# Dummy products in fp32, a re-ordered attention start and re-ordered loads in a fused attention and gated feed-forward kernel

## The chip, the cores and the metric

One core of a Trainium2 chip. The metric is the device time of one execution in microseconds (us). A profile is one execution; its span is 1.7 to 1.8 us shorter than the time that is measured for the same execution.

Names used here: PE is TensorE (matrix products), PEld its weight loads, DVE VectorE, ACT ScalarE, POOL GpSimd. POOL also issues the loads that convert fp32 in memory to bf16 on chip.

## The reference, cut to what matters

```python
# q, k, v: (8 batches, 8 heads, 1024, 64); E, F: (64, 1024)
k_proj = einsum('ks,bhsd->bhkd', E, k)
v_proj = einsum('ks,bhsd->bhkd', F, v)
scores = q @ k_proj^T / 8
attn   = exp(scores - max) / sum          # the kernel leaves the max out
x      = (attn @ v_proj) as (8192, 512)
g      = x @ w_gate                       # 512 x 1536
out    = (g * sigmoid(g)) * (x @ w_val) @ w_out
```

## The kernel before

The rows are cut into 16 chunks of 512. Each chunk goes through 12 steps f of the gate and val products (g and v, 128 columns of the weights each, 512 rows) and through the y products with `w_out`. The attention of later chunks is spread between these products. Only the start differs: nothing can be multiplied with the weights until the first chunk's attention is done, and that is a chain of small steps on four engines. It begins with turning E (to turn is to transpose, on PE) and projecting K, and the chunk is taken in two halves of 256 rows to start sooner.

The names in the code and in the profiles: the chunk's attention is cut into four parts, u = 0 to 3 (two groups of four heads, each for two halves of the rows). Each part has its scores, their exponentials ee, and AA, which is ee divided by its row sums (one multiplication with the reciprocals rr). AT is AA turned; BD and BDV hold the projections of K and V; P V is the product of BDV and AT; its turned result xT is the input of the gate and val products.

```python
ps_g, ps_v: 2 PSUM banks each;  ps_y: 1 bank;  ps_a: 3 banks      # banks "g", "v", "y", "a"

def load_w_gv(c0, c1, which=(0, 1)):      # one load of gate, one of val, issued by POOL
    ...
def u_V0(p0, p1, at):                     # V's projection for head pairs p0..p1 of batch 0
    t = bank(at, [P, p1 - p0, P], FP32, "kvp")
    matmul(out=t, lhsT=zeros[:, 0:P], rhs=zeros[...], start=True, stop=False)   # zero product
    for j in range(NJ):
        for c in range(2):                # two column halves of the array
            matmul(out=t[64*c:64*c+64, :, 64*c:64*c+64], lhsT=FT[:, j, :], rhs=..., start=False, ...)
    nc.scalar.copy(out=BDV[0][:, p0:p1, :], in_=t[:])

def warm(n):                              # n dummy products, to release the clock
    ps = bank("v", [P, CW], FP32, "warm")
    for _ in range(n):
        matmul(out=ps[:], lhsT=zeros[:, 0:P], rhs=zeros[:], start=True, stop=True)   # bf16, 512 columns

# the start, in program order (loads on POOL, everything else as named)
load_q(0, 0, (2, 4)); load F; load_v(0, (0, 4, 6, 8)); load_w_gv(0, 1); load_w_gv(1, 2, (0,))
warm(11); turn(0, "v"); warm(4)           # turn(0): E, turn(1): F
... K's first four heads: casts, u_KV, u_T, u_KT0, warm(1)
u_S(0, 0); u_R(0, 0); u_N(0, 0)           # scores+exp (PE, ACT), sum (DVE), scale = AA (POOL)
load_w_gv(1, 2, (1,)); load_w_gv(2, 4, (0,))
u_T(0, 2); warm(2); K's other heads; warm(1); u_KT0((2, 4)); u_T(0, 1); u_T(0, 3)
u_S(0, 2); u_R(0, 2); u_N(0, 2); turn(1, "a", (0,))
u_S(0, 1); u_R(0, 1); u_N(0, 1); turn(1, "a", (1,))
u_S(0, 3, "v"); u_R(0, 3)
u_A(0, 0, act); u_N(0, 3, dve)            # u_A: turn AA, copy by the named engine
u_V0(0, 2, "y"); u_PV2(0, 0, 0, 0, act); u_V0(2, 3, "y"); u_A(0, 2, act); u_V0(3, 4, "v")
u_PV1(...pair 2); u_A(0, 1, dve); u_PV1(...pair 3); u_A(0, 3, act)
load_w_gv(2, 4, (1,))
f_mm(0, 0, 0, 0); u_PV2(...); f_mm(0, 0, 1, 0); f_mm(0, 1, 0, 0); u_PV2(...); f_mm(0, 1, 1, 0)
load_w_gv(4, 6); load_q(0, 1, hs=(0, 4)); load_w_gv(6, 8); load_q(0, 1, hs=(4, 8)); load_w_gv(8, 10) ...
```

The softmax here doesn't subtract the row's maximum and nothing guards it: scores larger than these inputs give would overflow.

## Time and profile before

| | before |
|---|---|
| median of the first runs (568.65 to 569.04) | 568.66 us |
| span of the profile | 566.9 us |
| PE busy | 560.2 us, 99% |
| start of the third val product (T) | 25.93 us |
| start of the val product of f=6 | 33.29 us |
| DMA rate 22 to 30 us | 196 to 197 GB/s |

In a timeline line the first number is the start in us, the second the stretch in us; then come engine, line, operation, output and inputs, and how many instructions were merged. A bracket tells how long the engine was idle before and what ended it. In the view by stretches, a row has the stretch, its length and the busy time of PE, PEld, DVE, ACT and POOL with the number of instructions, then the granted clock, the DMA share and the DMA rate in GB/s. These are rows of before, first K's first projection, the first gate product and the third val product (T) from the timeline, then three stretches:

```profile
8.16 1.06 PE L150 MATMUL kvp<-kb,ET 128*64 128x256 bf16 x8
...
20.70 0.60 PE L377 MATMUL gps<-xT,wg 128*128 128x256 bf16 x4
...
25.93 1.03 PE L377 MATMUL vps<-xT,wv 128*128 128x512 bf16 x4
```

```profile
20.00:22.00 2.00, 1.82 (x21) 1.52 (x19) 1.19 (x3) 0.96 (x2) 2.00 (x4) 1.00 1.58 191
22.00:24.00 2.00, 1.98 (x19) 1.62 (x18) 1.28 (x4) 0.88 (x2) 2.00 (x4) 1.00 1.45 197
24.00:26.00 2.00, 1.90 (x14) 1.17 (x13) 1.56 (x3) 0.90 (x2) 1.37 (x2) 1.00 1.45 196
```

Before, the DMA rate stays at 191 GB/s or more from 20 to 30 us.

### The profile page before, as it was taken

To read this page: it belongs to the slowest core of one execution; us is meant where nothing else is said; L and a number is where in the kernel's file an instruction comes from. 1 tells how busy PE (TensorE), PEld (TensorE's weight loads), DVE (VectorE), ACT (ScalarE), POOL (GpSimd) and SP (SyncE) were. 2 spreads that over 40 slices of the span, in tenths; PEclk is the share of its full clock that TensorE was granted. 3 is DMA by queue.
4 is the path that set the end of the run, shared out by engine and by line. 5 is a ranking of instruction groups with operands and counts; after the bars stand their busy time and mean duration, and the time that the engine had idled before them with its cause. 6 is when DMAs were issued, how large, how long until landed. Compare 5 with 4: busy or idle time off the path is not lost.

```text
span 566.9 us, 7938 instructions
## 1 busy us (share of the span) xinstructions
PE 560.2 (99%) x2970; PEld 266.3 (47%) x2970; DVE 339.2 (60%) x576; ACT 236.0 (42%) x417; POOL 110.4 (19%) x124
## 2 busy tenths in 40 slices
PE   8999999999999999999999999999999999999997
PEld 4654444444444444444444444444444444444444
DVE  3786664766476645766466655666547665545550
ACT  3664352444435433443434434354343543443222
POOL 6851250124012400124002230023100220000000
PEclk9999999999999999999999999999999999999999
DMA  9999989729913795029940499105990214100012
GB/s 201 194 200 188 175 126 199 141 57 187 192 50 74 113 196 119 38 57 163 183 83 37 76 185 204 38 19 101 200 183 20 57 38 75 38 37 32 25 38 93
DMA packets 111159, 62.78 MB, mean 111 GB/s; under 512 B 64272, under 2 KB 102416, under 8 KB 111120
## 3 DMA queue, kind: packets, MB, share of 16 engines
q0 software_dynamic: 42896, 29.49, 36.1%
q1 hardware_dynamic: 67392, 31.46, 26.2%
q10 hardware_dynamic: 832, 1.31, 0.8%
q8 instruction: 23, 0.38, 0.3%
q14 instruction: 16, 0.13, 0.1%
HBM read 60.29 MB, written 16.78 MB: 136 GB/s over the span
## 4 chain that ended last, share of the span: by engine, by line
PE 97%; ACT 1%; DVE 1%; issue 0%
PE gps L377 29%; PE yps L415 29%; PE vps L377 29%; PE kvp L150 3%; PE sc L271 2%; PE pv L328 2%; PE warm L513 1%; ACT ee L275 0%; ACT AT L138 0%; DVE BD L138 0%; ACT th L389 0%; PE qTp L237 0%; PE efp L501 0%; PE aTp L317 0%; PE pv L343 0%
## 5 line engine op out<-in xcount | busy, mean ns | idle before, releaser
L396 DVE SCALAR_TENSOR_TENSOR s<-th,gps 128x512 f32<-128x512 f32 x192 | 130.3, 679 | 134.4 <-ACT th L389 134.0
L377 PE MATMUL gps<-xT,wg 128*128 128x512 bf16 (+1 forms) x776 | 197.6, 377 | 0.1
L377 PE MATMUL vps<-xT,wv 128*128 128x512 bf16 (+1 forms) x776 | 197.5, 377 | 0.0
L415 PE MATMUL yps<-wo,hT 128*128 128x512 bf16 (+1 forms) x780 | 194.5, 376 | 0.0
L389 ACT ACTIVATE th<-gps 128x512 f32<-128x512 f32 x192 | 114.6, 597 | 159.0 <-PE gps L377 153.9
L401 DVE TENSOR_TENSOR hT<-s,vps 128x512 bf16<-128x512 f32 x192 | 131.9, 687 | 20.4 <-DVE s L396 0.5
L301 POOL TENSOR_TENSOR AAd<-ee,rr 128x512 bf16<-128x512 f32 x56 | 58.2, 1041 | 342.5 <-issue 180.6
L415 PEld LDWEIGHTS <-hT 128*128 128x128 bf16 x780 | 76.2, 98 | 89.9
L377 PEld LDWEIGHTS <-wv 128*128 128x128 bf16 x776 | 74.0, 98 | 83.3 <-issue 2.9
L377 PEld LDWEIGHTS <-wg 128*128 128x128 bf16 x776 | 74.0, 98 | 81.3 <-issue 1.2
L425 ACT ACTIVATE ysb<-yps 128x512 f32<-128x512 f32 (+1 forms) x65 | 38.4, 590 | 77.7 <-PE yps L415 77.7
L138 ACT CAST xT<-pv 128x512 bf16<-128x512 f32 (+1 forms) x62 | 35.9, 581 | 52.5 <-PE pv L328 50.3
L286 DVE TENSOR_REDUCE zz<-ee 128x8 f32<-128x512 f32 x64 | 43.4, 679 | 22.1 <-ACT ee L275 22.1
L275 ACT ACTIVATE ee<-sc 128x512 f32<-128x512 f32 x64 | 38.2, 597 | 19.8 <-PE sc L271 18.7
L271 PEld LDWEIGHTS <-qTd 128*128 128x128 bf16 x224 | 17.2, 98 | 13.2 <-DMA qTd<-qb 0.2
L328 PE MATMUL pv<-AT,BDV 128*128 128x512 bf16 x60 | 22.4, 379 | 0.1
L271 PE MATMUL sc<-BD,qTd 128*128 128x128 bf16 x224 | 21.6, 219 | 0.0
L288 DVE RECIPROCAL rr<-zz 128x8 f32<-128x8 f32 x64 | 13.0, 203 | 6.6 <-DVE zz L286 0.5
L108 POOL DMA_DIRECT2D qb<-in_q_dram x18 | 16.3, 907 | 1.4 <-POOLq L651 0.8
L150 PE MATMUL kvp<-kb,ET 128*64 128x512 bf16 (+1 forms) x72 | 15.5, 358 | 0.0
L162 DVE CAST BDV<-kvp 64x256 bf16<-64x256 f32 x7 | 3.0, 426 | 20.0 <-ACT ks L158 17.8
L150 PE MATMUL kvp<-vb,FT 128*64 128x512 bf16 x56 | 13.4, 382 | 0.0
(66 smaller groups left out, 137.6 us busy)
## 6 DMA issues: line engine op xcount, KB each, us to landing
out_dram<-ysb SPq DMA_DIRECT2D x63, 256.0 KB, 2.3
qb<-in_q_dram POOLq DMA_DIRECT2D x14, 512.0 KB, 18.1
kb<-in_k_dram POOLq DMA_DIRECT2D x7, 1024.0 KB, 11.0
vb<-in_v_dram POOLq DMA_DIRECT2D x7, 1024.0 KB, 14.5
wo<-in_moe_w_out_dram POOLq DMA_DIRECT2D x2, 768.0 KB, 21.9
wg<-in_moe_w_gate_dram POOLq DMA_DIRECT2D x5, 256.0 KB, 8.4
wv<-in_moe_w_val_dram POOLq DMA_DIRECT2D x5, 256.0 KB, 9.0
kraw<-in_k_dram ACTq DMA_DIRECT2D x2, 512.0 KB, 4.9
```

The source lines that it names most:

```text
L138: (nc.scalar.copy if eng is nc.scalar else eng.tensor_copy)(out=out, in_=in_)
L150: nc.tensor.matmul(out=t[lo : lo + 64, h0:h1].rearrange("p h d -> p (h d)"), lhsT=w[:, j, :], rhs=src[b][:, h0:h1, j, :], start=(j == 0), ...
L271: nc.tensor.matmul(out=ps[:, n, :], lhsT=t[:, n, :], rhs=BD[b % 2][:, 4 * g + n, :], start=True, stop=True)
L275: nc.scalar.activation(out=e[:].rearrange("p h j k -> p (h j k)"), in_=ps[:].rearrange("p a k -> p (a k)"), func=AF.Exp, scale=scale,)
L286: nc.vector.reduce_sum(out=z[:], in_=e[:], axis=AX.X)
L301: eng.tensor_tensor(out=a.rearrange("p j h k -> p h j k"), in0=ee.pop((b, u))[:], in1=rr.pop((b, u))[:].unsqueeze(3).to_broadcast([P, 4, 2 ...
L377: nc.tensor.matmul(out=ps[:, ts], lhsT=(wg, wv)[w][:, kt, f * P : (f + 1) * P], rhs=x[:, kt, ts], start=(kt == 0), stop=(kt == NKT - 1),)
L389: nc.scalar.activation(out=th[:], in_=ps[:], func=AF.Tanh, scale=0.5)
L396: nc.vector.scalar_tensor_tensor(out=s1[:], in0=th[:], scalar=1.0, in1=g[:], op0=ALU.add, op1=ALU.mult)
L401: nc.vector.tensor_tensor(out=hT[c][:, f, :], in0=s1[:], in1=ps[:], op=ALU.mult)
L415: nc.tensor.matmul(out=yy[c][:, cs], lhsT=hT[c][:, f, i * P : (i + 1) * P], rhs=wo[:, f, cs], start=(f == 0), stop=(f == NFT - 1),)
L425: nc.scalar.activation(out=ysb[:, cs], in_=yy[c][:, cs], func=AF.Copy, scale=0.5)
```

## The change

Its intent is to shorten the start. The dummy products become a few long fp32 ones, presumably to have fewer instructions. Half of F's turn moves ahead into a dummy's place, with its copy on DVE. V's projection for the first two pairs becomes a wide form without the zero product (a memset on DVE in the first microseconds clears the target instead) and stands ahead of P V. The fourth AA moves from DVE to POOL and one copy from ACT to DVE. The third g is put in y's idle bank. The weights of f=2 and f=3 are loaded apart, those of f=3 behind the fourth AA on POOL, and the second half of the second chunk's q goes ahead of the weights of f=6 and 7.

```diff
+    def u_V0w(p0, p1, at):
+        t = bank(at, [P, p1 - p0, 2, D], FP32, "kvp")
+        for j in range(NJ):
+            nc.tensor.matmul(out=t[64:P]..., lhsT=FT[:, j, :], rhs=vb[0][:, 2 * p0 : 2 * p1, j, :], ...)
+        for c in range(2):
+            nc.scalar.copy(out=BDV[0][rows, p0:p1, rows], in_=t[64:P, :, c, :])
 ...
-            half[c, f, w] = bank("gv"[w], [P, CW], FP32, "gv"[w] + "ps")
+            where = "y" if (c, f, w) == (0, 2, 0) else "gv"[w]
+            half[c, f, w] = bank(where, [P, CW], FP32, where + "ps")
 ...  (warm(n): one fp32 product of min(64 n, 512) columns where n >= 4; its zeros come
      from a new fp32 memset; later warm(1) and warm(2) become warm(4) and warm(4))
-        warm(11)
+        for n in (8, 8, 4):
+            warm(n)
         turn(0, "v")
-        warm(4)
+        warm(8)
 ...
-        load_w_gv(2, 4, (0,))
+        load_w_gv(2, 3)
 ...
-        warm(1)                          # after K's other heads
+        turn(1, "a", (0,), dve)
 ...
+        turn(1, "a", (1,))               # ahead of the scores of u=2
-        turn(1, "a", (0,))               # and both turns of F out of their old places
-        turn(1, "a", (1,))
         u_S(0, 3, "v")
         u_R(0, 3)
+        u_N(0, 3)
+        load_w_gv(3, 4)
         u_A(0, 0, act)
-        u_N(0, 3, dve)
-        u_V0(0, 2, "y")
+        u_V0w(0, 2, "y")
+        u_V0(2, 3, "v")
         u_PV2(0, 0, 0, 0, act)
-        u_V0(2, 3, "y")
-        u_A(0, 2, act)
-        u_V0(3, 4, "v")
+        u_A(0, 2, dve)
+        u_V0(3, 4, "y")
 ...
+        f_mm(0, 0, 0, 0)                 # ahead of u_A(0, 3)
         u_A(0, 3, act)
-        load_w_gv(2, 4, (1,))
-        f_mm(0, 0, 0, 0)
 ...
         load_q(0, 1, hs=(0, 4))
+        load_q(0, 1, hs=(4, 8))
         load_w_gv(6, 8)
-        load_q(0, 1, hs=(4, 8))
```

More of the change, by code (lines that the diff above doesn't have):

```diff
@@ L185, in u_V0 @@
         nc.scalar.copy(out=BDV[0][:, p0:p1, :], in_=t[:])
+    def u_V0w(p0, p1, at):
+        t = bank(at, [P, p1 - p0, 2, D], FP32, "kvp")
+        for j in range(NJ):
+            nc.tensor.matmul(
+                out=t[64:P].rearrange("p a c d -> p (a c) d"),
+                lhsT=FT[:, j, :],
+                rhs=vb[0][:, 2 * p0 : 2 * p1, j, :],
+                start=(j == 0),
+                stop=(j == NJ - 1),
+            )
+        for c in range(2):
+            rows = slice(64 * c, 64 * c + 64)
+            nc.scalar.copy(out=BDV[0][rows, p0:p1, rows], in_=t[64:P, :, c, :])
     def u_KT(b, at="a", prs=(0, NPAIR)):
@@ L490 @@
         load_k(0, 4, 8)
-        zeros = const.tile([P, CW], BF16, name="zeros")
+        zero32 = const.tile([P, CW], FP32, name="zero32")
+        nc.vector.memset(zero32[:], 0.0)
+        zeros = const.tile([P, 2 * P], BF16, name="zeros")
         nc.vector.memset(zeros[:], 0.0)
@@ L495, with turn @@
         nc.vector.memset(ks[0][64:P], 0.0)
-        def turn(which, at, halves=(0, 1)):
+        nc.vector.memset(BDV[0][:, 0:2], 0.0)
+        def turn(which, at, halves=(0, 1), eng=nc.scalar):
             for half in halves:
@@ L506, in turn @@
                 js = slice(4 * half, 4 * half + 4)
-                copy(nc.scalar, (ET, FT)[which][:, js, :], ps[:])
+                copy(eng, (ET, FT)[which][:, js, :], ps[:])
         def warm(n):
             ps = bank("v", [P, CW], FP32, "warm")
-            for _ in range(n):
+            z = zeros if n < 4 else zero32
+            for _ in range(n if n < 4 else 1):
                 nc.tensor.matmul(
-                    out=ps[:], lhsT=zeros[:, 0:P], rhs=zeros[:],
+                    out=ps[:, 0 : min(64 * n, CW) if n >= 4 else 2 * P],
+                    lhsT=z[:, 0:P],
+                    rhs=z[:, 0 : min(64 * n, CW) if n >= 4 else 2 * P],
                     start=True, stop=True,
@@ L537 @@
         u_KT0((0, 2), "vg", (dve, dve, dve, act))
-        warm(1)
+        warm(4)
         u_S(0, 0, "g")
@@ L542 @@
         load_w_gv(1, 2, (1,))
-        load_w_gv(2, 4, (0,))
+        load_w_gv(2, 3)
         u_T(0, 2, "a", act)
-        warm(2)
+        warm(4)
         u_KV(0, "k", (4, 8), at="y")
-        warm(1)
+        turn(1, "a", (0,), dve)
         u_KT0((2, 4), "vg", (dve, dve, act, act))
```

## The prediction

> **What bounds the kernel now.** I read the page first: its busy line, its slices and the chain that ended last.
>
> ```profile
> PE 560.2 (99%) x2970; PEld 266.3 (47%) x2970; DVE 339.2 (60%) x576; ACT 236.0 (42%) x417; POOL 110.4 (19%) x124
> PE   8999999999999999999999999999999999999997
> PE 97%; ACT 1%; DVE 1%; issue 0%
> ```
>
> TensorE is the bound: 97% of the chain is its own work, and only the first slice (14.2 us) has an 8. The waits by window say the same: from 25 us on, TensorE has no wait on another engine, and the stretches 60 to 530 us are 100% busy. The change touches no product after the start, so it can move the time only through the moment at which the dense stream begins. I call that moment **T**: the start of the third val product (f=2, 512 columns), 25.93 us now. From there each f costs 1.73 us (25.07 to 26.80) without a gap. T earlier by x makes the kernel faster by x, unless a transfer stops the stream later.
>
> Next I read the timeline from 0 to 35 us, then the waits of TensorE there. Whatever precedes T is a chain of short steps over four engines:
>
> ```profile
> 1.20 4.88 PE L513 MATMUL warm<-zeros 128*128 128x512 bf16 x11 [1.20 <-DVE zeros L492]
> 6.12 1.07 PE L501 MATMUL efp<-ident_fp,Eraw 64*128 64x64 f32 x8
> ...
> 15.43 0.37 ACT L138 COPY FT<-efp 128x256 bf16<-128x256 bf16 x1
> ...
> 16.17 0.39 ACT L138 COPY FT<-efp 128x256 bf16<-128x256 bf16 x1
> ...
> 16.56 0.64 PE L178 MATMUL kvp<-vb,FT 128*64 128x128 bf16 x16
> ...
> 17.38 0.45 ACT L185 CAST BDV<-kvp 128x256 bf16<-128x256 f32 x1
> ...
> 17.88 0.39 PE L343 MATMUL pv<-AT,BDV 128*128 128x256 bf16 x2 [0.68 <-ACT BDV L185]
> ```
>
> The reader is to see two copies of F's turn on ACT among the exponentials, and P V waiting 0.68 us for the V projection's copy on the same engine. ACT runs without pause from 14.94 to 17.83 us in the chain.
>
> The third view is the issue list, taken around single issues, beside the timeline's issue times. It gives landings: issue plus time to landing.
>
> ```profile
> wv<-in_moe_w_val_dram POOLq DMA_DIRECT2D x1, 128.0 KB, 12.5
> ```
>
> ```profile
> 8.65 0.75 POOL L118 DMA_DIRECT2D wv<-in_moe_w_val_dram  x1
> 21.36 0.60 PE L377 MATMUL vps<-xT,wv 128*128 128x256 bf16 x4
> ...
> 22.34 0.42 PEld L377 LDWEIGHTS <-wv 128*128 128x128 bf16 x4
> ...
> 33.29 1.03 PE L377 MATMUL vps<-xT,wv 128*128 128x512 bf16 x4
> ```
>
> So the first val weights land at 8.65 + 12.5 = 21.15 us and are used from 21.25 us: **no slack**. Likewise gate f=1 lands at 11.24 + 10.1 = 21.34, val f=1 at 14.26 + 7.7 = 21.96 (used 22.34), gate f=2,3 at 23.26, val f=2,3 at 24.63, gate/val f=6,7 at 30.0 and 31.35, the second half of the second chunk's q at 32.7.
>
> **What the Trainium skill says.**
> - "FP8 and Floating Point Precision", TensorE Precision Notes: true fp32 takes four passes through the array. So an fp32 product of 512 columns should last as long as four bf16 ones. The kernel before has no long fp32 product; no row here shows it.
> - "TensorE: Matmul & The Clock Gate", Part 1: the array runs at half rate until it has been busy for some 3.4 us. The trace agrees: the first dummy products start 0.43 us apart (2.02, 2.45, 2.88), later ones of the same size 0.216 us. The page's PEclk row shows full clock throughout and does not show this.
> - Same page, Part 3: products on different column groups of the array overlap. The trace agrees: 16 V products of 128 columns on two column halves take 0.64 us, (0.64 - 0.2)/15 = 29 ns each, about half of a 128-column product's 57 ns.
> - "DMA: Bandwidth & Descriptors", Specifications: pieces under 512 B run below line rate. The trace agrees weakly: with 256 B pieces the DMA moved 181 GB/s (18 to 20 us), with 512 B pieces 196 (26 to 28 us).
>
> **The change part by part.**
>
> 1. *Dummies.* Before: 11 x 0.427 = 4.7 us from 1.20. After: 512 + 512 + 256 fp32 columns x 4 passes = 5120 column steps, as many as 10 bf16 products: 4.27 us. They wait for a 128x512 fp32 memset, twice the 0.27 us one: start 1.46, end of streaming 5.73 against 5.89. E lands at 0.74 + 5.2 = 5.94, so its turn moves from 6.09 to about 6.0. The four after it become one fp32 product of equal length (0.86 us). The later ones are equal (2 x 0.216 = 0.43) or sit in the wait for BD that ends at 10.90. Sum: **-0.1 us**, hidden costs apart.
>
> 2. *F's turns.* The first half moves to about 13.1 us, in the place of a dummy product, with its copy on DVE (idle 0.78 us before 13.89). F lands at 5.00 + 8.1 = 13.1: just in time. The second half goes before the scores of u=2; it takes some 0.37 us of TensorE, 0.3 of it in the wait for BD, so those scores and ee of u=2 come 0.1 later, which eats the 0.1 of part 1. One ACT copy (0.26) leaves ACT's row of work and the other moves ahead of ee. ACT in sequence: ee x3 from 15.0 at 0.5 each to 16.55, AT to 17.05.
>
> 3. *V projection.* The wide form for pairs 0 and 1 is 8 products of 256 columns on one column half, 8 x 0.107 = 0.86 us, against 0.44 plus a 0.1 zero product: 0.3 us longer, but it starts about 15.9 where it started at 16.56, and runs beside the exponentials. V's first heads land at 5.66 + 9.9 = 15.56. Two 64-row copies of about 0.26 follow AT: BDV complete at 17.55 against 17.83. P V starts at **17.6 instead of 17.88**.
>
> 4. *After that.* AT of u=2 moves from ACT to DVE (0.4), pair 3's projection comes up behind it, AA of u=3 moves from DVE (18.10 to 19.23) to POOL (three AA in a row at 1.02 from 16.7: end 19.77). xT of pair 3 is ready about 19.8, and the first gate product ends at 19.9 instead of 21.3. So **the attention side gains about 1.0 us**. AA of u=3 is needed only after that product.
>
> 5. *Weights eat it.* The bytes ahead of val f=0, gate f=1 and val f=1 are the same, so they land at 21.15, 21.34 and 21.96 again. TensorE waits from about 20.4 to 21.2, then val f=0 (0.44), gate f=1 (0.44), P V (0.22), val f=1 (0.44) until 22.7. The last xT copy ends at about 23.0; the second halves follow to 24.6.
>
> 6. *Third g in y's bank.* It removes the wait for g's bank (24.82 to 25.07, 0.25 us), but the next val product needs v's bank, free after hT: th 23.48, s to 24.81, hT to 25.6. The bank gain alone is below 0.1. T becomes about **25.68: -0.25 us**.
>
> 7. *Order of loads.* Gate and val of f=2 land as now or sooner, f=3 by about 24.8, used at 27. Two more small pairs cost 4 x 0.04 = 0.16 us of DMA time (128 KB at 181 or 196 GB/s of the counted bytes). With q ahead, gate/val f=6,7 land at about 31.5 and 32.9. Gate is used at 32.2, val at 33.29: slack of 0.3 us after the shift of part 6 is almost nothing. So the load order caps the gain near 0.3 us.
>
> Sum: 568.66 - 0.25 = 568.4; I take 568.35, since val f=0 landed oddly late (gate f=0 at 18.8, 2.35 us before it, for 0.65 us of bytes) and might land sooner.
>
> **The rivals.**
> - *No weight wait*: val f=0 lands near 20.4, and the full 0.9 us reaches T. For it: the odd 2.35 us. Against: val f=6,7 then stops the stream at 32.9, so 0.3 to 0.5 remain. Time 568.0.
> - *The fp32 dummies cost more than four passes* (weight loads between passes not hidden, some 0.1 us each) or don't release the clock: K's projection comes 0.5 to 1 us late. The weights' slack of part 5 then absorbs most: 568.6 to 569.
> - *The loads become the bound*: q ahead of the weights stops TensorE at f=6 by more than was gained, if the extra small pieces cost more than 0.16 us. Time 568.8 to 569.3.
> - *F late*: F's turn now stands in TensorE's order at 13.1, where F lands; 0.3 us of lateness goes to K's second half and all that follows, mostly absorbed by part 5.
>
> **Range and chances.** All of these lie between -1.0 and +0.6 us; 2% is 11.4 us, and the whole start is 25 us, most of it needed anyway. Runs of before differ by 0.4 us. Predicted 568.35 us, range 567.7 to 569.0; faster by over 2%: 0.005, within 2%: 0.985, slower by over 2%: 0.01.
>
> **What would show it.** In the profile of after: few fp32 rows from about 1.46 us that end near 5.9 (part 1); F's turn at 13.1 with a DVE copy (2); P V at 17.6 (3); a first gate product at about 19.4 and then a TensorE wait before the first val product near 21.2 (4, 5); the third val product at 25.7 (6); no or a short wait at val f=6 near 33 (7). The prediction is wrong if the val weights come in early and the stream at f=6 isn't stopped (faster than 567.7), or if the clock stays at half rate after 6 us or a load stops the stream by over half a microsecond (slower than 569).

## The result, and the profile after

The changed kernel took 569.25 us (median of four runs: 571.2, 569.18, 568.6, 569.32) against 568.66 before (568.65, 569.04, 568.66, 568.67). The ratio is 1.0014 with a 95% interval of 0.999 to 1.0039, so within noise the same. A ratio is the mean time of one kernel's fast runs over the mean of the other's fast runs of the same rounds, so it is not quite the ratio of the medians. The forecast of 568.35 with a range of 567.7 to 569.0 missed the median by 0.9 us, and the spread of 2.6 us was not foreseen at all.

The profile after is that of the 571.2 us run. First the page: its busy line, PE's slices and the chain that ended last.

```profile
PE 559.8 (98%) x2900; PEld 267.5 (47%) x2954; DVE 339.5 (60%) x579; ACT 235.6 (41%) x416; POOL 112.9 (20%) x127
PE   8999999999999999999999999999999999999997
PE 95%; DMA 2%; POOL 1%; ACT 1%; issue 1%; DVE 0%
```

In the chain there is now DMA with 2% and POOL with 1%: a transfer and its issuer have come onto the path. (PE's count of records is smaller; the waits of 60 to 530 us show none on another engine for PE, and some product records can be missing from a trace.) Second, the timeline after, the lines that answer to those of before:

```profile
1.46 4.63 PE L536 MATMUL warm<-zero 128*128 128x512 f32 x6 [1.46 <-DVE zero L510]
...
6.02 1.14 PE L522 MATMUL efp<-ident_fp,Eraw 64*128 64x64 f32 x8
...
7.18 2.08 PE L536 MATMUL warm<-zero 128*128 128x512 f32 x2
...
9.19 1.92 PE L150 MATMUL kvp<-kb,ET 128*64 128x256 bf16 x8
...
15.52 0.29 DVE L138 COPY FT<-efp 128x256 bf16<-128x256 bf16 x1 [0.52 <-PE efp L522]
...
17.84 1.06 PE L191 MATMUL kvp<-vb,FT 128*64 128x256 bf16 x8
...
19.69 0.39 PE L358 MATMUL pv<-AT,BDV 128*128 128x256 bf16 x2 [0.26 <-ACT BDV L200]
```

An fp32 product leaves two records (six for the first three products). The one after E's turn took 2.08 us; before, four bf16 products took 1.02 there. K's first projection took 1.92 us; before, it took 1.06 from 8.16. So in this run the array was still at half rate until about 11 us, and what hangs on K comes 1.9 us late (the copy of K's result starts at 11.14 instead of 9.26). The granted clock of the record says 1.0 for this run. Third, the DMA rate by stretches and the place where PE stops:

```profile
20.00:22.00 2.00, 1.90 (x33) 1.42 (x32) 1.35 (x4) 1.22 (x3) 2.00 (x3) 1.00 1.63 162
22.00:24.00 2.00, 2.00 (x22) 1.82 (x21) 1.10 (x3) 0.86 (x2) 2.00 (x4) 1.00 0.37 34
24.00:26.00 2.00, 1.98 (x18) 1.62 (x17) 1.21 (x3) 1.26 (x3) 2.00 (x4) 1.00 1.28 120
```

```profile
26.94 1.02 PE L395 MATMUL vps<-xT,wv 128*128 128x512 bf16 x4
...
34.33 1.04 PE L395 MATMUL gps<-xT,wg 128*128 128x512 bf16 x4 [0.95 <-DMA wg<-in_moe_w_gate_dram]
...
35.70 1.04 PE L395 MATMUL vps<-xT,wv 128*128 128x512 bf16 x4
```

The queue ran dry (34 GB/s), and ten microseconds later PE waited for the gate weights of f=6. The issue of the weights of f=3 came too late for the queue: gate's was issued at 21.73 us and landed 3.4 us later, at 25.13, while the load ahead of it had landed at 23.18. (Before, the loads from f=3 on were issued 6 us or more ahead of their landing.)

The sum is simple. Let T be the start of the third val product, and S the stall between it and the val product of f=6, that is their distance less the 7.36 us of before (33.29 - 25.93). After: T = 26.94 (1.01 late), S = 35.70 - 26.94 - 7.36 = 1.40; 566.9 + 1.01 + 1.40 = 569.3, and the span is 569.4. The same sum holds for the profiles of all the runs below, within 0.1 us, except e5 and e13, where the text tells the rest.

So two suspects stood: **C**, the clock, released late and at a varying time with fp32 dummies; and **Q**, the DMA queue, run low because POOL issues the weights of f=3 and all later loads only after three AA in a row.

### The profile page after: what moved, and what is told of

Its sections match the earlier page's. It is cut to its first block, busy times and chain, and to the rows that moved or that the text cites. A ratio compares the mean times of both kernels' runs of the same rounds, so it can differ in the third digit from the quotient of the medians.

```text
span 569.4 us, 7860 instructions
## 1 busy us (share of the span) xinstructions
PE 559.8 (98%) x2900; PEld 267.5 (47%) x2954; DVE 339.5 (60%) x579; ACT 235.6 (41%) x416; POOL 112.9 (20%) x127
## 3 DMA queue, kind: packets, MB, share of 16 engines
q1 hardware_dynamic: 67392, 31.46, 25.5%
## 4 chain that ended last, share of the span: by engine, by line
PE 95%; DMA 2%; POOL 1%; ACT 1%; issue 1%; DVE 0%
PE yps L433 29%; PE vps L395 28%; PE gps L395 28%; PE kvp L150 3%; PE sc L286 2%; PE pv L343 2%; DMA wv<-in_moe_w_val_dram 2%; PE warm L536 1%; POOL wg L118 0%; ACT ee L290 0%; POOL wv L118 0%; POOL qb L108 0%; PE efp L522 0%; PE qTp L252 0%; POOL AA L316 0%
## 5 line engine op out<-in xcount | busy, mean ns | idle before, releaser
L395 PE MATMUL gps<-xT,wg 128*128 128x512 bf16 (+1 forms) x750 | 194.2, 377 | 1.9 <-DMA wg<-in_moe_w_gate_dram 1.0
L433 PE MATMUL yps<-wo,hT 128*128 128x512 bf16 (+2 forms) x763 | 191.8, 376 | 0.7
L290 ACT ACTIVATE ee<-sc 128x512 f32<-128x512 f32 x64 | 37.9, 596 | 19.7 <-PE sc L286 18.5
L286 PE MATMUL sc<-BD,qTd 128*128 128x128 bf16 x224 | 21.7, 219 | 0.1
```

Source lines behind the costliest of these rows:

```text
L286: nc.tensor.matmul(out=ps[:, n, :], lhsT=t[:, n, :], rhs=BD[b % 2][:, 4 * g + n, :], start=True, stop=True)
L290: nc.scalar.activation(out=e[:].rearrange("p h j k -> p (h j k)"), in_=ps[:].rearrange("p a k -> p (a k)"), func=AF.Exp, scale=scale,)
L395: nc.tensor.matmul(out=ps[:, ts], lhsT=(wg, wv)[w][:, kt, f * P : (f + 1) * P], rhs=x[:, kt, ts], start=(kt == 0), stop=(kt == NKT - 1),)
L433: nc.tensor.matmul(out=yy[c][:, cs], lhsT=hT[c][:, f, i * P : (i + 1) * P], rhs=wo[:, f, cs], start=(f == 0), stop=(f == NFT - 1),)
```

## The experiments

Sixteen runs in four sets, each set on a chip of its own with its own runs of before (medians 568.73 to 568.77); all outputs agreed with the reference. The table has, for each profile, T, the stall S and the span, and all measured times. "Changed" is the changed kernel.

| run | kernel | T | S | span | times (us) | ratio to before (95%) |
|---|---|---|---|---|---|---|
| | before | 25.93 | 0 | 566.9 | 568.66 median | |
| | changed, first runs | 26.94 | 1.40 | 569.4 | 571.2, 569.18, 568.6, 569.32 | 1.0014 (0.999 to 1.0039) |
| e1 | changed, again | 25.36 | 0.46 | 566.8 | 568.6, 568.24, 568.93, 569.57, 568.86 | 1.0001 (0.9989 to 1.0014) |
| e2 | changed, bf16 dummies | 25.41 | 0.02 | 566.5 | 568.27, 569.29, 569.63, 569.19, 569.26 | 1.001 (0.9996 to 1.0024) |
| e3 | before, fp32 dummies | 25.77 | 0 | 566.7 | 568.5, 569.34, 568.84, 568.75, 568.71 | 1.0001 (0.9988 to 1.0013) |
| e5 | changed, q's half behind | 25.12 | 0.21 | 566.7 | 568.46, 568.46, 568.54, 568.5, 570.47 | 1.0001 (0.9989 to 1.0014) |
| e6 | changed, 4th AA on DVE | 25.47 | 0 | 566.4 | 568.2, 568.34, 570.1, 568.31, 570.01 | 1.0007 (0.9993 to 1.0021) |
| e7 | changed | 25.45 | 1.04 | 567.5 | 569.24 | |
| e8 | as e2 | 25.23 | 2.10 | 568.4 | 570.14 | |
| e9 | e2 with both edits of e5, e6 | 25.40 | 0 | 566.4 | 568.2, 568.5, 568.01, 568.11, 568.02 | 0.9986 (0.9974 to 0.9998) |
| e10 | e2 with e6's edit | 25.21 | 0 | 566.2 | 568.05, 568.46, 568.12, 568.05, 568.3 | 0.9986 (0.9974 to 0.9998) |
| e11 | e6 again | 25.27 | 0 | 566.3 | 568.04, 568.09, 568.12, 570.08, 568.22, 569.99 | 0.9996 (0.9982 to 1.0011) |
| e12 | e9, third g in g's bank | 25.53 | 0 | 566.6 | 568.33, 568.34, 568.13, 567.97, 568.33 | 0.9986 (0.9973 to 0.9999) |
| e13 | e10 without first dummies | 28.07 | 0 | 569.6 | 571.38, 571.11, 569.8, 571.35 | 1.0032 (1.0013 to 1.0051) |
| e14 | e10, dummies 0.54 us later | 25.92 | 0 | 566.9 | 568.64, 569.1, 568.4, 568.14, 568.65 | 0.9994 (0.9981 to 1.0006) |
| e15 | e6 | 25.98 | 0 | 566.9 | 568.72 | |
| e16 | e6 | 27.38 | 0.25 | 568.6 | 570.39 | |

(e4, a measurement with a much longer start, is told below.)

### Set 1: is it the dummies?

**e1**, the changed kernel unaltered:

> The changed kernel once more, for its spread. Seen so far: 571.2, 569.18, 568.6, 569.32 us. Theory C (the fp32 dummy products release the half-rate clock late and at a varying time): the times spread again over 1 us or more, and the profiled run shows half-rate products after 7.2 us. Rival Q (the loads that POOL issues behind three AA products run the DMA queue dry): the times are alike within 0.3 us and about 569.2, with a TensorE wait for a weight transfer near 30 us in any run.

The times spread over 1.3 us, but K's first projection ran at full rate in the profile (1.06 us), so C does not explain this profile. Nor is it quite what the rival expected: the times are not alike, and the stall is under half a microsecond. The profile shows the attention side of the change doing what was hoped for, and a small stall behind:

```profile
17.84 0.39 PE L358 MATMUL pv<-AT,BDV 128*128 128x256 bf16 x2 [0.26 <-ACT BDV L200]
...
19.41 0.89 PE L395 MATMUL gps<-xT,wg 128*128 128x256 bf16 x4
...
25.36 1.02 PE L395 MATMUL vps<-xT,wv 128*128 128x512 bf16 x4
```

The first gate product starts at 19.41 where before it started at 20.70, and T is 25.36 instead of 25.93, 0.57 us sooner; the stall S of 0.46 gives most of it back (566.9 - 0.57 + 0.46 = 566.8).

**e2**, the changed kernel with the dummies of before:

```diff
-        for n in (8, 8, 4):
-            warm(n)
+        warm(11)                # bf16, 512 columns each
         turn(0, "v")
-        warm(8)
+        warm(4)
 ...                             # later: warm(1) and warm(2) instead of warm(4) and warm(4)
```

> The changed kernel with the dummy products of before (11, 4, 1 and 2 bf16 ones), all else as changed. Theory C: the spread falls under 0.4 us, K's first products (8 of 256 columns) take about 1.06 us, not 1.92, and the time is 568.0 to 568.6. Rival Q: the time stays at 569 or above, with a dip of the DMA rate below 150 GB/s between 20 and 30 us.

The profiled run is good (568.27), the other four are 569.2 to 569.6, median 569.26. The spread did not fall: **C falls as the main cause** of the common loss. (The dip below 150 GB/s that the rival forecast is not in the profile either, where the lowest rate is 165; but it is the profile of the one short run.)

**e3**, the kernel before with the fp32 dummies alone (the reverse of the edit of e2):

> The kernel before with the fp32 dummy products alone. Theory C: slower than before by 0.3 to 2 us and spread over 1 us or more; where a profile shows K's first products at half rate (1.9 us), they start about 9.2 us instead of 8.16. Rival Q: 568.5 to 568.9, as before, no spread.

Median 568.75 against 568.73 for before in the same set, times 568.5 to 569.34. The fp32 dummies alone cost nothing in these five runs.

**e4**, a measurement, twelve fp32 products of 512 columns ahead of E's turn in the kernel of e3:

```diff
-        for n in (8, 8, 4):
+        for n in (8,) * 12:
```

> A measurement: the kernel before with twelve 512-column fp32 dummy products ahead of E's turn, to see when their spacing falls from about 1.7 us to about 0.86 us. Theory C (fp32 products count less for the release): the spacing stays at 1.7 us for far more than 6 us, perhaps for all twelve (to about 22 us). Rival (the release only comes at a chance moment[...]): the spacing halves before 8.3 us.

The weight loads of the dummies in e4, two to a product:

```profile
5.89 0.34 PEld L517 LDWEIGHTS warm<-zero 128*128 128x128 f32 x1 [0.52 <-issue]
6.74 0.34 PEld L517 LDWEIGHTS warm<-zero 128*128 128x128 f32 x1 [0.52 <-issue]
7.42 0.19 PEld L517 LDWEIGHTS warm<-zero 128*128 128x128 f32 x1 [0.34 <-issue]
7.85 0.19 PEld L517 LDWEIGHTS warm<-zero 128*128 128x128 f32 x1 [0.24 <-issue]
```

The distance is 0.85 us up to 6.74 and 0.43 from 7.42 on. So fp32 products alone did release the clock, near 7.2 us, some 5.7 us after their start. This is the rival's outcome (the spacing halves before 8.3 us) and a miss of C as it was written there, that fp32 products count less. What is left of C is that the release is late in some runs. It also gives the price of one: 2 x 0.43 = 0.86 us at full rate against 0.216 for bf16, four passes, as predicted. The time of 577.55 us says nothing more; the start was made longer on purpose.

### Set 2: is it the loads?

**e5**, q's second half behind the weights of f=6 and 7 again:

```diff
         load_q(0, 1, hs=(0, 4))
-        load_q(0, 1, hs=(4, 8))
         load_w_gv(6, 8)
+        load_q(0, 1, hs=(4, 8))
```

> The changed kernel with the second half of q behind the weights of f=6,7 again. Theory Q (late loads stop the stream at f=6): the weights of f=6 land about 1.3 us sooner (30.4 and 31.8 us instead of 31.74 and 33.18), the two short waits of TensorE for them go, the times fall to 568.0 to 568.4 and the spread to under 0.5 us. Rival J (the spread comes from elsewhere, the start or the end of the run): median near 568.9 and spread over 1 us as in the changed kernel.

Four times within 0.08 us (568.46 to 568.54), and one of 570.47. The weights of f=6 landed at 31.36 and 32.69 instead of 31.74 and 33.18, 0.4 to 0.5 us sooner than in e1 where 1.3 was expected, as the whole queue was late in this run too (163 to 173 GB/s from 22 to 28 us). And q now came late: its turn started at 34.03 after a wait for it, 0.23 us later than the scores ahead of it allow. Up to the next gate product e5 lost 0.49 us in all, against e9 below (34.27 - 25.12 against 34.06 - 25.40), which gives 566.9 - 0.81 + 0.49 = 566.6. Part of the loss went from the weights to q. So **the order of the loads is not the whole cause**: four of the five times are better than most of e1's, but the loads are late as a whole, whichever stands last.

**e6**, the fourth AA on DVE and the copy on ACT as before, so that the weights of f=3 are issued one AA sooner:

```diff
-        u_N(0, 3)
         load_w_gv(3, 4)
         u_A(0, 0, act)
+        u_N(0, 3, dve)
 ...
-        u_A(0, 2, dve)
+        u_A(0, 2, act)
```

> The changed kernel with the fourth AA on VectorE and its neighbour copy on ScalarE, as before, so that POOL issues the weights of f=3 about 1.0 us sooner. Theory Q: those issues start at about 18.9 us instead of 19.9, the DMA rate between 22 and 28 us rises from 161-172 to over 185 GB/s, weights of f=6 land about 0.4 us sooner; the start of the third val product may move back by 0.2 to 0.4 us; time 568.4 to 568.8, spread smaller. Rival J: spread as in the changed kernel.

POOL's timeline in e1, then in e6:

```profile
16.89 3.04 POOL L316 TENSOR_TENSOR AA<-ee,rr 128x512 bf16<-128x512 f32 x3 [0.31 <-ACT ee L290]
19.88 0.81 POOL L118 DMA_DIRECT2D wg<-in_moe_w_gate_dram  x1
```

```profile
16.85 2.04 POOL L316 TENSOR_TENSOR AA<-ee,rr 128x512 bf16<-128x512 f32 x2 [0.30 <-ACT ee L290]
18.84 0.81 POOL L118 DMA_DIRECT2D wg<-in_moe_w_gate_dram  x1
```

One AA less on POOL, 1.04 us, and every later load is issued that much sooner. The DMA rate from 24 us on, e1 first, then e6:

```profile
24.00:26.00 2.00, 1.92 (x11) 0.95 (x10) 1.80 (x3) 1.20 (x2) 2.00 (x4) 1.00 1.28 163
26.00:28.00 2.00, 2.00 (x11) 0.93 (x10) 1.89 (x3) 0.60 (x1) 2.00 (x3) 1.00 1.37 172
```

```profile
24.00:26.00 2.00, 1.98 (x13) 1.06 (x11) 1.90 (x3) 1.11 (x2) 2.00 (x4) 1.00 1.46 196
26.00:28.00 2.00, 2.00 (x11) 0.88 (x9) 1.79 (x4) 0.68 (x2) 1.39 (x3) 1.00 1.46 197
```

The weights of f=6 land at 31.40 and 32.74, 0.3 to 0.4 us sooner than in e1. The profile has no stall (S = 0), although q's half is still ahead of the weights, and T moved back by only 0.11 us against e1. (From 22 to 24 us the rate was 183 GB/s, just under the 185 that were forecast.) Three times are 568.2 to 568.34. But two are near 570.

**e7** and **e8** are meant to catch a long run in a profile.

> One more look at the changed kernel, to catch a run at 569 us or above in a profile. Theory Q: where the time is 569 or above, TensorE waits for weights between 30 and 36 us for over 0.8 us in total. Rival J: no such wait, the time lies before 20 us or after 540 us.

> One more look at the changed kernel with bf16 dummy products (four of its five times were 569.2 to 569.6), to catch such a run in a profile. Theory Q: TensorE waits for weights between 30 and 36 us for over 0.8 us in total. Rival J: no such wait; the loss lies elsewhere.

Both did: 569.24 and 570.14 us, each with K's first projection at full rate (1.06 us), and each with PE waiting for the weights of f=6. In e8 its weight loads show it:

```profile
32.10 0.55 PEld L395 LDWEIGHTS <-wg 128*128 128x128 bf16 x4 [0.62 <-DMA wg<-in_moe_w_gate_dram]
...
34.68 0.55 PEld L395 LDWEIGHTS <-wv 128*128 128x128 bf16 x4 [1.50 <-DMA wv<-in_moe_w_val_dram]
```

In e8 the stall is 2.1 us with T at 25.23, so 566.9 - 0.70 + 2.10 = 568.3 (span 568.4). In e7 it is 1.04 us with T at 25.45: 567.5. **Q holds for the common loss of 0.5 to 1 us.** That the unprofiled times of 569.2 to 569.6 of the changed kernel and of e2 are of this kind is likely, but only argued: their profiles do not exist.

In e8 some 1.2 of the 2.1 us look different. Its val weights of f=6 landed 2.53 us after the gate weights (34.61 and 32.08); in every other profile of the table the distance is 1.33 to 1.44. In that gap, from 32.3 us, the DMA engines also moved a single packet of another queue, which the view of the DMA queues from 32 to 33 us names q8, kind instruction:

```profile
q8 instruction: 1, 0.02, 5.8%
```

The 5.8% are a share of the 16 DMA engines over the stretch from 32 to 33 us, so the packet held one engine for 0.93 us. Every profile of the table has such a packet, at 31.5 us (before) to 37.5 us (e13), and another at 18.5 to 21.7 us. In e1, e2, e7, e13 and e16 a transfer just behind the later one lands 0.9 to 1.1 us late too, but after the weights of f=6, where it stops nothing; in before, e5 and e14 no transfer does. So it is likely that in e8 the packet fell into the one transfer without slack. No run moved it, so this is not shown.

### Set 3: the version that the runs point to, and the times near 570

**e9** is the changed kernel with the edits of e2 (bf16 dummies), e6 (fourth AA on DVE) and e5 (q behind):

> The version that the runs point to: the changed kernel with bf16 dummy products, the fourth AA on VectorE, q behind the weights of f=6,7. Theory Q+C (late loads cost up to 1.8 us at f=6; an unreleased clock costs some 1.7 us in some runs with fp32 dummies): all five times within 0.4 us, 568.0 to 568.4, no TensorE wait for a weight after 25 us, none of the 570 us kind. Rival (the 570 us kind has nothing to do with the dummies' type): one or two of five times at 569.9 or above.

568.01 to 568.5 (0.1 us above what was written at the upper end), median 568.11, against 568.77 for before: the ratio of 0.9986 has an interval that ends below 1, a gain of 0.14%, far under the 2% from which a run is called faster. There is no wait for a weight after 25 us and no time near 570.

**e10** is the same with q's half ahead, as in the change (the edit of e5 left out):

> The same with q ahead of the weights of f=6,7, as in the change. Theory Q+C: no times of the 570 us kind; but the weights of f=6 land about 1.3 us later than in the version with q behind and only just in time (31.4 and 32.7 us), so some times may be 0.2 to 0.5 us longer: 568.1 to 568.8. Rival: one or two of five at 569.9 or above.

Median 568.12, the same. With the queue kept full, the place of q's half costs nothing; the feared half microsecond did not come. e10 is also the cleanest test of Q: it differs from e2 by the edit of e6 alone, and its five times are 568.05 to 568.46 where four of e2's five are 569.19 to 569.63. (The two ran on different chips, with before at 568.77 and 568.73.)

**e11** is e6 once more, for the times near 570:

> The version with the fourth AA on VectorE and fp32 dummies once more (before: 568.2, 568.34, 570.1, 568.31, 570.01). Theory C: one to three of five times near 570 again, and if the profile catches one, its K projection (8 products) takes 1.9 us instead of 1.06 and the third val product starts near 27.0 us instead of 25.47. Rival: the times near 570 are gone, or come with K's projection at full rate.

Two of six are near 570 again (570.08, 569.99), four are 568.04 to 568.22. The profiled one is a short run. The only edit between e10 and e11 is the dummies' type.

**e12** is e9 with the third g back in g's bank:

```diff
-            where = "y" if (c, f, w) == (0, 2, 0) else "gv"[w]
+            where = "gv"[w]
```

> The version of the first run of this set with the third g back in g's own bank. My step 6: the bank is worth under 0.1 us, as the next val product waits for hT anyway: the third val product starts 0 to 0.1 us later, time 568.0 to 568.5. Rival: the whole wait of 0.25 us that the bank removes comes back.

T is 25.53 against 25.40 and 25.21 in e9 and e10; the median is 568.33 against 568.11, but the times overlap (567.97 to 568.34). Counted from the last 256-row val product, which takes the rest of the start out, T comes 1.56 us later in e12 (25.53 - 23.97) and 1.49 in e9 and e10 (25.40 - 23.91, 25.21 - 23.72): the bank is worth 0.07 us, and a wait of 0.25 us did not come back.

### Set 4: are the times near 570 an unreleased clock?

**e13** takes the dummies ahead of K's projection out of e10, so that the clock cannot be released in time:

```diff
-        warm(11)
         turn(0, "v")
-        warm(4)
```

> The version with bf16 dummies and the fourth AA on VectorE, with the 11 and the 4 dummy products before K's first projection taken out. Theory C: E's turn and K's first projection run at half rate (8 products in about 1.9 us instead of 1.06), the clock is released a few us later, the third val product starts 0.3 to 1.8 us later than 25.21, times 568.5 to 570.2. Rival: K's projection is no slower and the time is 568.1.

```profile
6.04 1.11 PE L520 MATMUL efp<-ident_fp,Eraw 64*128 64x64 f32 x8 [6.04 <-DMA Eraw<-in_E_dram]
8.01 1.86 PE L150 MATMUL kvp<-kb,ET 128*64 128x256 bf16 x8 [0.86 <-DVE kb L138]
```

K's projection takes 1.86 us, T is 28.07, the times are 569.8 to 571.38. Against the 568.12 of e10, an unreleased clock costs 1.7 to 3.3 us here, more than I expected. (T alone gives 566.9 + 2.14 = 569.0; of the other 0.6 us of the span, 0.3 is a wait for a turned q between 60 and 300 us, and the rest was not traced.)

**e14** is e10 with an extra memset ahead of the zeros, so that the bf16 dummies start at 1.73 us:

```diff
+        late = const.tile([P, CW], FP32, name="late")
+        nc.vector.memset(late[:], 0.0)
         zeros = const.tile([P, CW], BF16, name="zeros")
```

> The version with bf16 dummies and the fourth AA on VectorE, with an extra memset of 128x512 fp32 ahead of the zeros, so that the dummies start later than with fp32 (about 1.7 us). If the later start makes the 570 us kind: one to three of five times at 569.9 or above. If the fp32 type makes it: all five 568.0 to 568.5.

No time near 570, though the start is later than that of the fp32 dummies (1.46). The times of 568.14 to 569.1 are as a chain that starts 0.54 us later would give; three of the five (568.64, 568.65, 569.1) are outside what I wrote. So there is **no sign that the later start makes the times near 570**. Five runs can't exclude it: at 7 long runs in 33, five have none with a chance of 30% (0.79 to the fifth power). That the fp32 type matters rests on the counts below.

**e15** and **e16** are e6.

> A look at the version with fp32 dummies and the fourth AA on VectorE, to catch a time near 570 (4 of 11 so far). Theory C: if it is near 570, K's first projection takes 1.9 us and the third val product starts near 27 us, and the run has no other loss; if it is near 568.2, K's projection takes 1.06 us. Rival: near 570 with K's projection at 1.06 us.

> The same look once more, with the same expectations: near 570 with K's first projection at 1.9 us, or near 568.2 with 1.06 us (theory C); near 570 with 1.06 us (rival).

e15 took 568.72 us: K at 1.06 us, but E landed late (PE waited 0.43 us for it, until 6.52). e16 took 570.39 and is what was looked for:

```profile
7.23 2.07 PE L536 MATMUL warm<-zero 128*128 128x512 f32 x2
9.24 1.88 PE L150 MATMUL kvp<-kb,ET 128*64 128x256 bf16 x8
11.05 0.40 PE L252 MATMUL qTp<-ident_bf,qb 128*128 128x128 bf16 x4
```

K at half rate, T at 27.38, hardly a stall (0.25). The first turn of q, behind, is at full rate. The run at 571.2 had the same start. So **C holds for the times near 570**, in the two of them that have a profile with fp32 dummies; for the other five it is argued from their times alone.

How often: of 33 executions with fp32 dummies (changed 4, e1, e3, e5, e6 five each, e7, e11 six, e15, e16), 7 took 569.9 us or more. Of 26 changed executions with bf16 dummies (e2, e8, e9, e10, e12, e14) one did, e8, and there the profile shows the loads. Before itself had two of 42 (570.39 and 570.56), but both with a granted clock of 0.997 in the record, where all the others have 0.999 or 1.0; what those are is open, as no profile of one exists.

The fairest comparison is within the versions with the fourth AA on DVE: 5 of 13 times are near 570 with fp32 dummies (e6, e11, e15, e16), none of 20 with bf16 ones (e9, e10, e12, e14). If the type did not matter, all five would fall among the 13 with a chance of about 0.5%.

## Why the prediction was wrong

**Part 1, the dummies.** The size of the products was right: 4 passes, 0.86 us (e4), E's turn at 6.02. The reading of the clock was not complete: the prediction took over 3.4 us to the release and said that the trace agrees, but in that very trace all eleven dummies run at half rate, until 4.9 us after their start; only the rates agree. What failed is that the release of the clock was taken as given ("Sum: -0.1 us"). In 7 of 33 executions it came too late or the run was long for another reason; in the two profiled, K came 1.9 us late. The rival that names it was sized at "568.6 to 569", with most "absorbed"; it costs 570 to 571.2, as lateness of K also delays POOL's loads.

**Part 2, F's turns.** Right. In e1 the first half runs at 13.19 us with its copy on DVE, the exponentials follow one another from 15.19.

**Part 3, V's projection.** The form took 1.06 us with the pipeline's end, close to the 0.86 of streaming that was reckoned, and started at 15.99 in e1. But AT ended at 17.24, not 17.05, and P V started at 17.84, not 17.6, so the projection moved P V by almost nothing (17.88 before).

**Part 4, the attention side.** The first gate product started at 19.41 in e1, where "about 19.4" was written, 1.29 us earlier than before. But this part moved the fourth AA to POOL and looked only at when AA was needed. **It did not ask what stood behind it on POOL: the issue of every later load.** This is the omission that led to the miss.

**Part 5, the weights' wait.** Half right. The first val weights landed at 19.1 to 20.9 us in the changed versions, not 21.15, as the rival with the odd 2.35 us said. This has little to do with the change: in e3, with the loads of before, they landed at 19.26. One packet of q8 (see e8) passes near 19 us in both, so chance is a likely reason for the odd 2.35 us. Gate f=1 landed at 20.7 to 21.3 in the runs with a full-rate start, about as written. So T was 25.1 to 25.5 in most of these runs instead of 25.68: 0.4 to 0.8 us of gain, not 0.25.

**Part 6, the bank.** Right: 0.07 us (e12).

**Part 7, the loads.** This is the step that failed. It added 0.16 us for two more small pairs and took the queue as full, so that the weights of f=6 "land at about 31.5 and 32.9". They landed at 31.74 and 33.18 (e1), 32.38 and 33.81 (e7), 32.08 and 34.61 (e8, with bf16 dummies), because the queue ran at 139 to 165 GB/s from 22 to 26 us instead of 196 (e10, with the same small pieces but the earlier issue, ran at 187 and 195; in e8 the late transfer told above comes on top). In e1 the landings are level with before up to val of f=3 (24.58 against 24.63) and 0.4 us behind from gate of f=4 on (26.32 against 25.93). The stall of 0.46, 1.04 and 2.10 us took back the gain at T of 0.57, 0.48 and 0.70. Two of its sums are off as well: a small pair costs 0.055 us more, not 0.04 (131 kB at 181 against 196 GB/s), so 0.22 for four; and the slack of val f=6 by its own figures is 33.29 - 0.25 - 32.9 = 0.14 us, not 0.3. It was said rightly that f=6 is where the stream would stop and that there was "almost nothing" of slack; the size of the lateness was wrong, and its cause, the issue behind three AA, was not seen. In e1 the lateness is only 0.28 us (33.18 against 32.9), and the stall is larger because T came 0.32 us sooner than forecast; in e7 the lateness is 0.9 us. The prediction's rivals had both outcomes: a stop at f=6 that leaves 0.3 to 0.5 us of gain, and a stop that costs more than was gained (568.8 to 569.3), the latter put down to small pieces. The order of q and weights, on which the part dwelt, does not matter once the queue is full (e9 and e10).

Where the expected gain went is then settled for the profiled runs: it was there at T, and it was given back seven microseconds later. Not settled is why the lateness varies so much between runs of one kernel: e2 had almost no stall and e8 2.1 us, with the same code. Of that, 1.2 us are the late transfer beside the packet of q8, and POOL's issues came 0.26 us later in e8 (19.72 against 19.46). Why fp32 dummies release the clock less reliably stays open.

## What to carry to other kernels

An engine that both computes and issues loads must be read in both roles: moving one 1.04 us operation to POOL kept no product waiting for it, and starved the DMA queue behind it. When a chain that feeds a saturated engine is shortened, check the landing time of everything that this engine will ask for in the next ten microseconds, under the new issue times and not the old ones, and leave slack. And a kernel whose times spread needs profiles of its long runs: the two kinds of long run here had different causes and were told apart only by looking again.

## What the Trainium skill lacked or had wrong

- "TensorE: Matmul & The Clock Gate", Part 1, gives a warm-up budget of about 3.4 us, with half a microsecond of variation, and adds that one kernel had 6, 11 or 14 half-rate products in different runs; it has nothing on the type of the operands. Here all eleven dummy products of before ran at half rate, until 6.08 us (4.88 us from their start), which fits the addition and not the budget; in e4 the release came some 5.7 us after the start, and in e16 and the 571.2 us run near 11 us, some 9.5 us after the start of fp32 dummies, with PE busy nearly all the time. Of 33 executions with fp32 dummies 7 took 569.9 us or more, of 26 with bf16 dummies one, for another reason. And the granted clock was recorded as 1.0 for the run whose first 11 us were at half rate: only the spacing of the products showed it.
- "DMA: Bandwidth & Descriptors", Why small descriptors are slow, reckons 27% overhead for 256 B pieces. Reckoned in the same way, pieces of 512 B have 3 cycles in 19, 16%, so the rate with 256 B should be 14% lower, an estimate from that page. In a stretch with almost only small pieces (18 to 20 us, before: 259 B on average) the DMA moved 181 GB/s against 196 with larger ones (24 to 26 us: 492 B): 8%.
- No page that I read has a figure for how a late issue starves the queue: here 1.04 us of delay on POOL took the DMA rate from 196 to 163 GB/s for two microseconds (e6 against e1, 24 to 26 us).
- No page that I read has a figure for what a packet of the instruction queue costs the loads beside it: here one held one of 16 DMA engines for 0.93 us, and the transfer beside or behind it landed 0 to 1.2 us late (the later packet of each profile; read from traces, not tested).
